# Attention by 256 tokens, weights in 1 MB pieces, second expert matrix and output in blocks of 320 and 192 columns

## The chip, the cores and the metric

One core of a Trainium2 chip runs the kernel. The metric is device time in microseconds (us) of one execution; lower is better. An execution of the kernel before took 193.95 us in the median of three runs (192.44 to 196.75).

## The reference

Chunked attention with memory keys, followed by a soft mixture of experts. Inputs are float32, and the sizes are: 4 batches, 8 heads, 768 tokens, head size 64; 3072 tokens of 512 channels for the experts; 8 experts with 4 slots each and 1024 hidden units.

```python
for c in range(nc):                                   # 24 chunks of 32 queries per batch
    k_ctx = k[:, :, max(0, 32*c - 16):min(S, 32*c + 32 + 8)]
    k_full = concatenate([mem_k, k_ctx], axis=2)      # 8 memory keys + at most 56
    a = softmax(scale * q_c @ k_full.T)
    out[:, :, c_start:c_end] = a @ v_full
x = out.transpose(0, 2, 1, 3).reshape(3072, 512)
logits = x @ phi                                      # 3072 x 32 slots
d = softmax(logits, axis=0)                           # over all tokens
slot_input = d.T @ x                                  # 32 x 512
for e in range(8):                                    # 4 slots of expert e
    slot_out[e] = relu(slot_input[e] @ w1[e]) @ w2[e] # 512x1024, then 1024x512
y = softmax(logits, axis=1) @ slot_out                # 3072 x 512
```

The inputs of the attention are 6.3 MB each for q, k and v, the two expert matrices 16.8 MB each, the output 6.3 MB.

## The kernel before, in words

**Attention.** `NU` = 24 units of 128 tokens. Of each unit, four chunks of 32 queries lie on the four column groups of TensorE, so that 16 matmuls of 128 columns make the scores (`s`, line 218), and 16 the product with the values (`a`, line 271). Two heads share the 128 partitions: even rows hold one head, odd rows the other, so every load of keys or values goes to every second partition (64 rows), once per head. Chunks overlap in their keys. The value windows of odd chunks have half of their keys in common with those of the even chunk: a copy on VectorE or ScalarE in turn (`share_v`, line 129) fills that half, in partitions 0 to 63, and a load of 32 rows (`vx`, in `load_v`, line 123) the other half, in partitions 64 to 127. Between the two products stand the row maximum, the subtraction, the exponential, the row sum and its reciprocal (VectorE and ScalarE), and transposes by TensorE (`pt`, and `xt` of the result for the logits). Every four units the logits (`l`, 16 matmuls of 128 columns) and the running sum over tokens (`D`, 4 matmuls of 512 columns) follow.

**Experts.** The slot inputs (`si`, copied to `siT`) are ready after the last unit. `expert_in` (line 484) multiplies them with `w1` of two experts at a time (`h`), `expert_out` (line 529) with one half of the columns of `w2` (`so`, 256 columns, two blocks). Between these stand the softmax over slots and its transposes (`combine_weights`, line 470, with a copy on GpSimd). `combine` (line 557) forms the output of one block (`o`), and six stores of 512 KB each write it.

**Transfers.** All of them are issued by SyncE (SP), in one order that the program fixes, and SP waits for each one's target buffer before it issues it; what stands behind waits as well. Weights come in pieces of 512 KB into `NW` = 13 buffers of their own during the attention (`load_w`, line 161, paced by `WRATE`), and into the attention's buffers as these are given up (`freed`, line 148). A piece can be loaded again into a buffer only when the piece before it has been used.

**Order of the work.** The loop over units (line 362) is written as a pipeline: in step `i` TensorE does the transposes of unit `i`, the scores of unit `i+2`, the result transposes of `i-1`, then the values of `i`. Each engine keeps the order in which its instructions are written (`InOrder`, line 56); the copies of GpSimd (POOL) at lines 115 and 473 do not belong to that rule. All instructions of a wrapped engine have the line of the helper (L66), so rows are told apart by the names of tiles.

Of the kernel before, what the change touches and what calls it, by code (L numbers as in the profile page):

```python
# [11 lines left out]
F32R = mybir.dt.float32r  # L12
# [4 lines left out]
P = 128  # L17
# [3 lines left out]
NKEY = NMEM + LEFT + CHUNK + RIGHT  # L21
CPU = P // CHUNK
UPB = S // P
NU = B * UPB
HALF_U = 3
NHALF = NU // HALF_U
SPAN_STEP = CPU // 2 * (NMEM + 2 * CHUNK)
SPAN_EXTRA = LEFT + RIGHT
STREAM = (S // CHUNK // 2) * (NMEM + 2 * CHUNK) + SPAN_EXTRA
HALF_W = HALF_U * SPAN_STEP + SPAN_EXTRA  # L30
# [3 lines left out]
E = 8  # L34
SPE = NSLOT // E
F = 1024
NG = NU // 4
NBLK = 2
WB = DM // NBLK
# [3 lines left out]
PIECE = 1024  # L43
NW = 13
NV = 3
W0 = 1
SHARE_MOD = 2
SHARE_DVE = 1
WARM0 = 3
FILL = (4, 2, 6, 2, 2)  # L50
WARM1 = 1
WRATE = 0.9
WSTART = 2


class InOrder:
    """An engine whose instructions keep the order in which they are written."""
# [13 lines left out]
def window_start(c):  # L71
    return (c // 2) * (NMEM + 2 * CHUNK) + (c % 2) * CHUNK


@with_exitstack
def tile_attn_softmoe(
# [3 lines left out]
    kT: bass.AP,  # L80
    vw: bass.AP,
    vx: bass.AP,
# [6 lines left out]
    pe, dve, act, sp = (InOrder(tc, e) for e in (nc.tensor, nc.vector, nc.scalar, nc.sync))  # L89
    cp = ctx.enter_context(tc.tile_pool(name="cp", bufs=1))  # L90
    wk = ctx.enter_context(tc.tile_pool(name="wk", bufs=2))
    ps = ctx.enter_context(tc.tile_pool(name="ps", bufs=2, space=bass.MemoryType.PSUM))

    k_slab = [cp.tile([P, 2, NPAIR, HALF_W], F32, tag=f"k{i}", name=f"k{i}") for i in range(2)]
    v_slab = [cp.tile([P, 2, 2, 2, 2, NPAIR, D], F32, tag=f"v{i}", name=f"v{i}") for i in range(NV)]
    q_slab = [cp.tile([P, 2, NPAIR, P], F32, tag=f"q{i}", name=f"q{i}") for i in range(3)]
    x_slab = [cp.tile([P, 4, DM], F32, tag=f"x{i}", name=f"x{i}") for i in range(2)]
    w_slab = [cp.tile([P, PIECE], F32, tag=f"w{i}", name=f"w{i}") for i in range(NW)]
    lT = cp.tile([P, NG, P], F32, tag="lT", name="lT")
    c_sb = cp.tile([P, NU, NSLOT], F32, tag="c", name="c_sb")  # L100
    hT = cp.tile([P, E, NFC, NSLOT], F32, tag="hT", name="hT")
# [4 lines left out]
    phi_sb = cp.tile([P, NKC, NSLOT], F32, tag="phi", name="phi_sb")  # L106

    def load_q(p):
        sp.dma_start(q_slab[p % 3], qT[p])

    def load_k(hb, lo=0, hi=HALF_W):
        b, half = divmod(hb, 2)
        off = half * HALF_U * SPAN_STEP - LEFT
        if half and lo == 0:
            nc.gpsimd.tensor_copy(
                out=k_slab[1][:, :, :, 0:SPAN_EXTRA], in_=k_slab[0][:, :, :, HALF_W - SPAN_EXTRA:HALF_W]
            )
        lo = max(lo, SPAN_EXTRA if half else LEFT)
        hi = min(hi, HALF_W - RIGHT if half else HALF_W)
        for par in range(2):  # L120
            sp.dma_start(k_slab[half][par:P:2, par, :, lo:hi], kT[b, :, par, :, off + lo:off + hi])

    def load_v(p):
        for par in range(2):
            sp.dma_start(v_slab[p % NV][par:P:2, par, 0], vw[p, par])
        for par in range(2):
            sp.dma_start(v_slab[p % NV][64 + par:P:2, par, 1], vx[p, par])

    def share_v(u):
        v = v_slab[u // 2 % NV]  # L130
        src, dst = v[64:128, :, 0, u % 2], v[0:64, :, 1, u % 2]
# [5 lines left out]
    flat = {}  # L137
    for name, tiles, pat in (
        ("k", k_slab, "p a g n -> p (a g n)"), ("q", q_slab, "p u g n -> p (u g n)"),
        ("v", v_slab, "p a o u c g d -> p (a o u c g d)"), ("x", x_slab, "p u n -> p (u n)"),  # L140
    ):
        for i, t in enumerate(tiles):
            f = t.rearrange(pat)
            flat[name, i] = [f[:, o:o + PIECE] for o in range(0, f.shape[1] - PIECE + 1, PIECE)]
    slabs = list(w_slab)
    last = NU // 2 - 1
    freed = [(NU - 6, ("k", 0)), (NU - 6, ("q", (last - 2) % 3)), (NU - 5, ("q", (last - 1) % 3))]
    freed += [(NU - 5, ("v", (last - d) % NV)) for d in range(NV - 1, 1, -1)]
    freed += [(NU - 3, ("q", last % 3)), (NU - 3, ("k", 1)), (NU - 3, ("v", (last - 1) % NV))]
    freed += [(NU - 1, ("x", 0)), (NU - 1, ("v", last % NV)), (NU, ("x", 1))]  # L150
    usable = {i: NW for i in range(NU + 1)}
    for since, key in freed:
        slabs += flat[key]
        for i in range(since, NU + 1):
            usable[i] = len(slabs)

    pieces = [("w1", e, kc) for e in range(E) for kc in range(NKC)]
    pieces += [("w2", blk, e, h) for blk in range(NBLK) for e in range(E) for h in range(2)]
    where = {}

    def load_w(upto):
        for i in range(len(where), min(upto, len(pieces))):
            kind, *at = pieces[i]
            where[pieces[i]] = s = slabs[i % len(slabs)]
            if kind == "w1":
                sp.dma_start(s, w1[at[0]].rearrange("(p kc) f -> p kc f", kc=NKC)[:, at[1], :])
            else:
                sp.dma_start(s, w2[at[0], at[1], :, at[2]])

    def span(t):  # L170
        lo = 0 if t == 0 else t * SPAN_STEP + SPAN_EXTRA
        return lo, (t + 1) * SPAN_STEP + SPAN_EXTRA

    warm = cp.tile([P, 512], F32, tag="warm", name="warm")

    def warm_up(n):
        w_ps = ps.tile([P, 512], F32, tag="L", name="warm_ps", bufs=1)
        for _ in range(n):
            pe.matmul(w_ps, lhsT=warm[:, 0:P], rhs=warm, start=True, stop=True)

    def keep_warm(n):
        if n:
            w_ps = ps.tile([P, 512], F32, tag="S", name="fill_ps")
            for _ in range(n):
                pe.matmul(w_ps[:, 0:P], lhsT=warm[:, 0:P], rhs=warm[:, 0:P], start=True, stop=True)

    dve.memset(warm, 0.0)
    for lo, hi in (span(0), (span(0)[1], HALF_W)):
        for par, eng in ((0, dve), (1, nc.gpsimd)):
            eng.memset(k_slab[0][:, par, :, lo:hi], 0.0)  # L190
    make_identity(nc, ident)
    for i in range(NV):
        nc.gpsimd.memset(v_slab[i], 0.0)  # L193
    nc.gpsimd.memset(hT, 0.0)
    act.copy(
        out=k_slab[1].rearrange("p a g n -> p (a g) n"),
        in_=warm[:, 0:HALF_W].rearrange("p (o n) -> p o n", o=1).broadcast_to([P, 2 * NPAIR, HALF_W]),
    )
    warm_up(WARM0)

    load_q(0)
    sp.dma_start(phi_sb, phi.rearrange("(kc p) s -> p kc s", p=P))
    load_k(0, *span(0))
    load_k(0, span(0)[1])
    load_q(1)
    load_v(0)
    load_k(1)
    for p in range(1, NV):
        load_v(p)
        if p == 1:  # L210
            load_q(2)
    load_w(W0)
    dve.tensor_reduce(out=sel, in_=ident.rearrange("p (g s) -> p s g", s=NSLOT), axis=AX.X, op=ALU.add)
    dve.tensor_copy(out=gsum, in_=sel.rearrange("p (o s) -> p o s", o=1).broadcast_to([P, 4, NSLOT]))

    pexp, rz, xT = {}, {}, {}

    def scores(u):
        t = u % UPB
        k = k_slab[(u // HALF_U) % 2]  # L220
        base = (t % HALF_U) * SPAN_STEP
        s_ps = ps.tile([P, H, NKEY], F32, tag="S", name=f"s{u}")
        for g in range(NPAIR):
            for j in range(CPU):
                w0 = base + window_start(j)
                pe.matmul(
                    s_ps[32 * j:32 * j + 32, 2 * g:2 * g + 2, :],
                    lhsT=q_slab[u // 2 % 3][:, u % 2, g, 32 * j:32 * j + 32],
                    rhs=k[:, :, g, w0:w0 + NKEY],
                    start=True, stop=True,  # L230
                )
        return s_ps

    def softmax(u, s_ps):
        t = u % UPB
        if t == 0:
            dve.memset(s_ps[0:32, :, 0:LEFT], NEG)
        if t == UPB - 1:
            dve.memset(s_ps[96:128, :, NKEY - RIGHT:NKEY], NEG)
        mx = wk.tile([P, H, 1], F32, tag="mx", name=f"mx{u}")  # L240
        dve.tensor_reduce(out=mx[:, :, 0], in_=s_ps, axis=AX.X, op=ALU.max)
        p = wk.tile([P, H * NKEY], F32, tag="p", name=f"p{u}", bufs=3)
        dve.tensor_tensor(
            out=p.rearrange("p (g n h) -> p g h n", g=NPAIR, h=2),
            in0=s_ps.rearrange("p (g h) n -> p g h n", h=2),
            in1=mx.rearrange("p (g h) o -> p g h o", h=2).broadcast_to([P, NPAIR, 2, NKEY]),
            op=ALU.subtract,
        )
        pexp[u] = p
# [367 lines left out]
```

## Time and profile before

| what | value |
|---|---|
| time of the runs | 192.44, 193.95, 196.75 us |
| span of the profiled execution | 193.7 us |
| TensorE busy, share of the span | 154.5 us, 80% |
| VectorE, ScalarE, GpSimd busy | 63%, 40%, 10% |
| bytes moved | 63.1 MB, of which 56.4 MB read from HBM and 6.3 MB written |
| mean rate | 326 GB/s |
| mean granted TensorE clock | 0.942 |

How to read it: busy shares are means over stages that have different limits, so they are read by stage, and against the row of the DMA engines. In that row the share is that of the 16 DMA engines that hold a packet, and GB/s is what they moved. A full share at a lower rate means packets that take longer, not more data. "issue" in a chain of waits is time in which the engine waited for nothing that the profile shows.

### The profile page before, as it was taken

The page shows a single profiled execution, that of the slowest core. Times are in us where ns is not written, and L with a number is a line of the kernel's source. Part 1 is how long each engine was busy: PE and PEld are TensorE (multiplying, and loading weights), DVE is VectorE, ACT ScalarE, POOL GpSimd, SP SyncE. Part 2 cuts the span into 40 slices and gives each one's busy share as a digit, 9 for nine tenths or more (in the row PEclk, how much of TensorE's full clock was granted, in tenths as well). Part 3 has the DMA queues.
Part 4 walks back from the last instruction along what each step waited for, and adds up shares of the span by engine and source line. Part 5 has one row for each costly group of instructions (what it writes and reads, how often), then busy time and mean ns, then how long its engine had stood idle before and what let it go on. Part 6 is the DMA issues. An engine that isn't in the chain of part 4 may idle for free.

```text
span 193.7 us, 6125 instructions
## 1 busy us (share of the span) xinstructions
PE 154.5 (80%) x2637; PEld 108.0 (56%) x2637; DVE 122.1 (63%) x249; ACT 77.9 (40%) x137; POOL 19.4 (10%) x22
## 2 busy tenths in 40 slices
PE   6733997859996969989579996999899769599540
PEld 3313775737684737757457684767466535365330
DVE  4699999829999649989936997243742220370550
ACT  8003457415756434763445577220322220160240
POOL 8991000000000000000000000000311100000000
PEclk9995899978999999999978999999999978999995
DMA  5999969998899999889978999999999999999296
GB/s 154 305 276 285 287 188 292 343 320 298 278 279 329 344 337 326 254 271 354 261 231 240 335 394 418 409 405 409 412 405 409 409 407 408 409 415 401 85 376 273
DMA packets 21194, 63.11 MB, mean 326 GB/s; under 512 B 2992, under 2 KB 7600, under 8 KB 21168
## 3 DMA queue, kind: packets, MB, share of 16 engines
q1 hardware_dynamic: 21168, 62.73, 92.8%
q8 instruction: 21, 0.34, 0.8%
q14 instruction: 5, 0.04, 0.1%
HBM read 56.43 MB, written 6.29 MB: 324 GB/s over the span
## 4 chain that ended last, share of the span: by engine, by line
PE 45%; DMA 23%; DVE 15%; issue 7%; POOL 3%; ACT 2%; SPq 1%; POOLq 0%
PE s L66 8%; PE a L66 8%; DMA k<-in_kT_dram 6%; DMA w<-in_w_dram 5%; PE xt_ps L66 5%; DMA v<-in_w_dram 5%; DVE z L66 4%; PE h L66 4%; PE so L66 4%; PE pt_ps L66 4%; DMA v<-in_vx_dram 3%; PE o L66 3%; PE D_ps L66 3%; DMA v<-in_vw_dram 3%; DVE v L66 3%
## 5 line engine op out<-in xcount | busy, mean ns | idle before, releaser
L66 PE MATMUL s<-k,q 128*32 128x128 f32 x768 | 28.8, 291 | 6.6 <-issue 4.2
L66 PE MATMUL a<-v,pt 128*32 128x128 f32 x768 | 27.8, 281 | 1.9 <-ACT pt L66 1.1
L66 PEld LDWEIGHTS s<-k,q 128*32 128x32 f32 x768 | 22.1, 117 | 12.1 <-issue 9.9
L66 PEld LDWEIGHTS a<-v,pt 128*32 128x32 f32 x768 | 21.4, 113 | 8.3 <-issue 6.4
L66 ACT COPY xT<-xt_ps 128x512 f32<-128x512 f32 x24 | 14.0, 584 | 29.2 <-PE xt_ps L66 28.9
L66 ACT ACTIVATE p<-p 128x512 f32<-128x512 f32 x24 | 15.1, 629 | 25.1 <-DVE p L66 25.1
L66 PE MATMUL pt_ps<-ident,p 128*128 128x128 f32 x96 | 16.7, 299 | 6.2 <-ACT p L66 6.2
L66 PE MATMUL xt_ps<-ident,x 128*128 128x128 f32 x96 | 16.4, 293 | 6.0 <-issue 4.4
L66 DVE TENSOR_TENSOR x<-a,z 128x512 f32<-128x512 f32 x24 | 16.5, 688 | 5.6 <-PE a L66 5.1
L66 DVE TENSOR_REDUCE mx<-s 128x8 f32<-128x512 f32 x24 | 16.1, 670 | 5.2 <-PE s L66 4.9
L66 PEld LDWEIGHTS pt_ps<-ident,p 128*128 128x128 f32 x96 | 10.7, 147 | 11.7 <-issue 11.7
L66 DVE TENSOR_TENSOR p<-s,mx 128x512 f32<-128x512 f32 x24 | 16.6, 693 | 0.8
L66 ACT COPY pt<-pt_ps 128x512 f32<-128x512 f32 x24 | 13.9, 578 | 8.0 <-PE pt_ps L66 8.0
L66 DVE TENSOR_REDUCE z<-p 128x8 f32<-128x512 f32 x24 | 16.3, 681 | 0.8
L66 PEld LDWEIGHTS xt_ps<-ident,x 128*128 128x128 f32 x96 | 10.4, 143 | 11.1 <-issue 7.5
L66 ACT COPY v<-v 64x1024 f32<-64x1024 f32 x12 | 12.5, 1046 | 0.3
L193 POOL MEMSET v<- 128x4096 f32 x3 | 10.5, 3513 | 0.0
L66 PE MATMUL o<-shl,cst 128*128 128x256 f32 x48 | 7.6, 302 | 3.0 <-DVE shl L66 2.9
L66 DVE COPY so_sb<-so 128x256 f32<-128x256 f32 x2 | 0.8, 425 | 14.1 <-PE so L66 14.1
L473 POOL COPY c<-c_sb 128x512 f32<-128x512 f32 x6 | 3.6, 614 | 60.3 <-DVE c_sb L66 48.0
L66 PEld LDWEIGHTS o<-shl,cst 128*128 128x128 f32 x48 | 6.3, 189 | 4.8 <-ACT shl L66 3.6
L66 PE MATMUL D_ps<-x,dT 128*32 128x512 f32 x48 | 7.4, 604 | 1.8 <-issue 1.6
(101 smaller groups left out, 195.1 us busy)
## 6 DMA issues: line engine op xcount, KB each, us to landing
w<-in_w_dram SPq DMA_DIRECT2D x26, 512.0 KB, 9.1
v<-in_w_dram SPq DMA_DIRECT2D x16, 512.0 KB, 10.2
q<-in_qT_dram SPq DMA_DIRECT2D x12, 512.0 KB, 7.2
v<-in_vw_dram SPq DMA_DIRECT2D x24, 256.0 KB, 6.6
k<-in_w_dram SPq DMA_DIRECT2D x12, 512.0 KB, 9.5
out_dram<-v SPq DMA_DIRECT2D x8, 512.0 KB, 5.2
k<-in_kT_dram SPq DMA_DIRECT2D x8, 424.0 KB, 8.5
v<-in_vx_dram SPq DMA_DIRECT2D x24, 128.0 KB, 6.7
```

The costliest lines, as they stand in the source:

```text
L66: return self.tc.keep_in_program_order(f(*args, **kwargs))
L193: nc.gpsimd.memset(v_slab[i], 0.0)
L473: nc.gpsimd.tensor_copy(out=c4, in_=c_sb[:, 4 * G:4 * G + 4, :].rearrange("p u (o s) -> p u o s", o=1).broadcast_to([P, 4, 4, NSLOT]),)
```

## The change

- A unit is 256 tokens (12 units). Scores and values stay 128 columns wide per matmul; the maximum, the exponential and the sums go over twice as many columns.
- The loads of keys bring one contiguous row of 4.5 to 4.7 KB per partition in place of four of 1.7 KB. They carry the part that two chunks share; the first chunk's keys are copied by GpSimd (`first_k`).
- The shared half of the odd chunks' values is copied by GpSimd (`share_v`, 8 copies of 256 columns per unit), no more by VectorE and ScalarE. The other half is a load of 32 rows to every fourth partition (`load_new`). Units 0 to 2 load both halves from memory (`load_both`).
- SP's order in a step is: `load_new` of unit `i+2`, even values of `i+4`, q of `i+4`, k of `i+5`, one piece of weights.
- Weights are pieces of 1 MB: 8 buffers of their own, then the attention's. The second matrix is cut at column 320: 11 pieces for the first block, 7 for the second, each 0.98 MB but for the last of a block.
- The logits of four units of 128 are formed as partial sums (4 matmuls of 512 columns, a copy, 4 matmuls of 128 columns). The last group keeps the old form.
- The softmax over slots of the first 12 units of 128 tokens is done under the last attention steps, the rest behind the first two experts, without the copies of GpSimd.
- The output of the first block is formed between the matmuls of the second block, and the combine matmuls read 32 rows each, in float32, in place of 128 rows in fp32r.

The core of the diff:

```diff
+U = 256
+UPB = S // U
+BLK = ((0, 320, 6), (320, 192, 10))
-PIECE = 1024
-NW = 13
+PIECE = 2048
+NB = 3
+NQ = 2
+NE = 4
+NO = 3
+NW = 8
+EARLY_W = 2
+WLAST = 7
...
-    def load_v(p):
-        for par in range(2):
-            sp.dma_start(v_slab[p % NV][par:P:2, par, 0], vw[p, par])
-        for par in range(2):
-            sp.dma_start(v_slab[p % NV][64 + par:P:2, par, 1], vx[p, par])
+    def load_v(u):
+        for h in range(2):
+            sp.dma_start(even_v(u)[h:P:2, h], vw[u, 64 * h:64 * h + 64, 0])
+    def load_both(u):
+        e, o = u % NE, NE + u % NO
+        for h in range(2):
+            sp.dma_start(v_t[h:P:2, e:o + 1:o - e, h], vw[u, 64 * h:64 * h + 64])
...
-        if u % SHARE_MOD < SHARE_DVE:
-            dve.tensor_copy(out=dst, in_=src)
-        else:
-            act.copy(out=dst, in_=src)
+        for h in range(2):
+            for i in range(CP):
+                cols = slice(NPAIR * D * i, NPAIR * D * (i + 1))
+                pool.tensor_copy(out=odd_v(u)[:, h, cols], in_=even_v(u)[:, h, cols])
+    def load_new(u):
+        for h in range(2):
+            sp.dma_start(odd_v(u)[h:P:4, h], vw[u, 64 * h:64 * h + 64:2, 1])
...
+    for u in range(NU - NB, NU):
+        freed += [(2 * u - 3, k_t[u % NB].rearrange("p a n -> p (a n)")[:, 0:PIECE])]
+    freed += [(2 * NU - 5, q_t.rearrange("p a g n -> p (a g n)"))]
+    freed += [(2 * u, even_v(u).rearrange("p a n -> p (a n)")) for u in range(NU - NE, NU)]
+    freed += [(2 * u, odd_v(u).rearrange("p a n -> p (a n)")) for u in range(NU - NO, NU)]
...
+    for i in range(NU):
+        if i and i + 2 < NU:
+            load_new(i + 2)
+        if i >= 1:
+            transpose_x(i - 1)
+        if i + 1 < NU:
+            exponent(i + 1)
...
+        a_ps = values(i, pt)
+        if G is not None and first:
+            lp = partial_logits(G)
...
+        normalize(i, a_ps)
+        if i + NE < NU:
+            load_v(i + NE)
+        if i >= WLAST:
+            load_w(usable[2 * i])
...
+        rest = (lambda: sum_logits(G, lp)) if G is not None and first else None
+        if i + 2 < NU:
+            softmax(i + 2, scores(i + 2, between=rest))
...
+        if i + 1 < NU:
+            pt = transpose_p(i + 1)
+            normalizer(i + 1)
+        if i + 3 < NU:
+            first_k(i + 3)
+            share_v(i + 3)
+        if i and i + 4 < NU:
+            load_q(i + 4)
+        if i + 5 < NU:
+            load_k(i + 5)
+        load_w(min(NW, EARLY_W + i) if i < WLAST else usable[2 * i + 1])
...
+    expert_out(0, banks("so0", "S")[:, 0, 0:BLK[0][1]])
+    under = {0: lambda: sum_sets(0)}
+    for G in range(NG - 1):
+        under[G + 1] = lambda G=G: combine(0, G, True)
+    expert_out(1, row(BLK[1][1], "so1"), under)
+    combine(0, NG - 1, True)
+    sum_sets(1)
+    for G in range(NG):
+        combine(1, G, G % 2 == 1)
```

**How it moves instructions.** First SP in the middle of the attention. Names: q, k and v are the attention's inputs, vw and vx the two kinds of value windows, w the weights. Before, over 256 tokens:

```order
L66 DMA v_67<-in_vw_dram 64x1024 x2
L66 DMA v_67<-in_vx_dram 32x1024 x2
L66 DMA q_71<-in_qT_dram 128x1024
L66 DMA w_76<-in_w_dram 128x1024
L66 DMA k_65<-in_kT_dram 64x4x424 x2
L66 DMA w_77<-in_w_dram 128x1024
```

And now, one step:

```order
L67 DMA v<-in_vw_dram 32x1024 x2
L67 DMA v<-in_vw_dram 64x1024 x2
L67 DMA q<-in_qT_dram 128x1024
L67 DMA k_66<-in_k_dram 64x1152 x2
L67 DMA w_74<-in_w_dram 128x2048
```

The load of 32 rows now stands first, ahead of the even values, and a piece of weights has twice the size. Next GpSimd in the same steps, where nothing but one copy of keys per six units stood before:

```order
L67 COPY k_66<-k_65 128x2x4x24
L67 COPY k_66<-k_66 128x2x4x8
L67 COPY v<-v 128x256 x8
L67 COPY k_67<-k_66 128x2x4x24
L67 COPY k_67<-k_67 128x2x4x8
L67 COPY v<-v 128x256 x8
```

It has nine or ten copies per step, and `load_new` waits for the eight of its unit. Last TensorE near the end; so is the second matrix's product, r its sum over the four column groups, o the output. Before:

```order
L66 MATMUL so_2323<-k_65,hT 32x256 x12
L66 MATMUL r_2390<-so_sb_2388,gsum 128x256
L66 MATMUL o_0_0_2396<-shl_2392,cst_1992 128x256 x2
L66 MATMUL o_0_1_2400<-shl_2392,cst_1992 128x256 x2
L66 MATMUL o_1_0_2405<-shl_2392,cst_2052 128x256 x2
```

And now, inside the second block:

```order
L67 MATMUL so_2071<-v,p 32x192 x8
L67 MATMUL o_3_S<-xT,lT 128x320 x2
L67 MATMUL o_3_A<-xT,lT 128x320 x2
L67 MATMUL so_2071<-k_66,p 32x192 x8
L67 MATMUL o_4_S<-xT,lT 128x320 x2
L67 MATMUL o_4_A<-xT,lT 128x320 x2
L67 MATMUL so_2071<-k_66,p 32x192 x2
```

The first block's output now lies between the matmuls of the second block, where it stood ahead of all of them.

## Rows read from the trace of the kernel before

**Rows 1.** The page's 40 slices of the span: DMA share in tenths, rate.

```profile
DMA  5999969998899999889978999999999999999296
GB/s 154 305 276 285 287 188 292 343 320 298 278 279 329 344 337 326 254 271 354 261 231 240 335 394 418 409 405 409 412 405 409 409 407 408 409 415 401 85 376 273
```

**Rows 2.** Busy time by stage, us: PE, PEld, DVE, ACT, POOL; clock, DMA share, GB/s.

```profile
0.00:20.00 20.00, 11.24 (x104) 6.00 (x108) 15.43 (x15) 6.30 (x5) 14.69 (x13) 0.85 0.91 258
20.00:112.00 92.00, 78.71 (x1649) 58.65 (x1641) 74.10 (x159) 47.54 (x85) 1.04 (x3) 0.96 0.93 293
...
139.00:172.00 33.00, 28.44 (x381) 17.65 (x381) 11.01 (x26) 8.97 (x17) 2.46 (x4) 0.95 1.03 408
...
180.00:184.00 4.00, 2.43 (x14) 1.85 (x14) 2.14 (x5) 1.42 (x3) 0.00 (x0) 1.00 0.11 44
184.00:193.70 9.70, 2.08 (x14) 1.60 (x12) 2.57 (x4) 2.37 (x5) 0.00 (x0) 0.71 0.82 324
```

**Rows 3.** The same columns, short stretches inside the attention, by what was queued.

```profile
9.60:10.60 1.00, 1.00 (x29) 0.75 (x21) 1.00 (x1) 0.00 (x0) 1.00 (x2) 1.00 1.07 418
20.00:21.00 1.00, 1.00 (x28) 0.92 (x24) 0.93 (x4) 0.00 (x0) 0.00 (x0) 0.55 1.12 389
43.00:45.00 2.00, 2.00 (x26) 1.47 (x28) 1.66 (x3) 0.65 (x2) 0.00 (x0) 0.55 1.06 393
64.00:66.00 2.00, 2.00 (x53) 1.44 (x44) 1.43 (x3) 0.58 (x1) 0.00 (x0) 1.00 1.04 410
16.60:17.90 1.30, 0.35 (x2) 0.38 (x3) 1.26 (x3) 0.63 (x1) 0.00 (x0) 0.50 1.00 186
21.20:22.40 1.20, 1.20 (x30) 0.83 (x26) 1.17 (x3) 0.15 (x1) 0.00 (x0) 1.00 0.98 198
```

**Rows 4.** The page's DMA issues: count, KB each, median us to landing.

```profile
v<-in_vx_dram SPq DMA_DIRECT2D x24, 128.0 KB, 6.7
```

**Rows 5.** Chain of waits, 45 to 57 us: start, us, what; one unit's matmuls.

```profile
45.55 0.59 PE pt_ps L66 x4
...
46.25 1.01 PE s L66 x32
47.26 0.59 PE xt_ps L66 x4
47.84 1.01 PE a L66 x32
...
51.05 1.00 PE D_ps L66 x8
```

**Rows 6.** The same chain, 26 to 45 us: a wait for keys and the logits.

```profile
28.76 4.29 DMA k<-in_kT_dram
...
37.78 1.01 PE l L66 x32
```

**Rows 7.** The same chain, 122 to 194 us: end of the attention to the experts.

```profile
122.26 0.88 PE a L66 x32
...
132.90 0.29 DVE siT L66
...
139.07 3.59 PE h L66 x64
...
172.46 7.09 PE so L66 x128
```

**Rows 8.** Timeline from 0 to 24 us: start, us, engine, line, what.

```profile
6.25 6.96 POOL L193 MEMSET v<- 128x4096 f32 x2
...
20.27 1.36 PE L66 MATMUL a<-v,pt 128*32 128x128 f32 x32
```

**Rows 9.** Groups of instructions by form: busy us, mean ns, idle time before.

```profile
L66 DVE COPY gsum<-sel 128x128 f32<-128x128 f32 x1 | 8.3, 8291 | 0.0
...
L473 POOL COPY c<-c_sb 128x512 f32<-128x512 f32 x6 | 3.6, 614 | 60.3 <-DVE c_sb L66 48.0 <-PE ct_ps L66 12.3
...
L115 POOL COPY k<-k 128x192 f32<-128x192 f32 x4 | 1.4, 346 | 73.4 <-DMA k<-in_kT_dram 73.4
```

More of the change, by code (lines that the diff above doesn't have):

```diff
@@ L148, in tile_attn_softmoe @@
[L148 to L154, printed above, removed]
+    stats = cp.tile([P, 3, NG], F32, tag="stats", name="stats")
+    warm = cp.tile([P, P], F32, tag="warm", name="warm")
@@ L159, in tile_attn_softmoe @@
+    pieces += [("w2", blk, i) for blk, (_, _, per) in enumerate(BLK) for i in range(-(-E * NFC // per))]
+    first_w2 = {blk: pieces.index(("w2", blk, 0)) - 2 * E for blk in range(len(BLK))}
     where = {}
@@ L191, in tile_attn_softmoe @@
[L191 to L230, printed above, removed]
-                )
-        return s_ps
@@ L251, in exponent, with clear_k, clear_v @@
-    def exponent(u):
-        act.activation(out=pexp[u], in_=pexp[u], func=AF.Exp, scale=SCALE)
+                _, n, per = BLK[at[0]]
+                n *= min(per, E * NFC - per * at[1])
+                sp.dma_start(s[:, 0:n], w2[first_w2[at[0]] + at[1], :, 0:n])
+    def clear_k(eng, u, h, part=slice(0, KW)):
+        eng.memset(k_t[u][:, h, part], 0.0)
+    def clear_v(eng, t, halves=range(2)):
+        for h in halves:
+            if eng is act:
+                act.copy(out=t[:, h], in_=warm[:, 0:1].broadcast_to([P, VW]))
+            else:
+                eng.memset(t[:, h], 0.0)
@@ new lines, in tile_attn_softmoe @@
+    dve.memset(warm, 0.0)
+    for h in range(2):
+        clear_k(dve, 0, h, slice(0, KW // 2))
+        clear_k(pool, 0, h, slice(KW // 2, KW))
+    clear_k(dve, 1, 0)
+    clear_k(pool, 1, 1)
+    for u in range(NDIRECT):
+        clear_v(act, even_v(u))
+    clear_v(dve, odd_v(0), [0])
+    clear_v(pool, odd_v(0), [1])
+    clear_k(dve, 2, 0)
+    clear_k(pool, 2, 1)
+    load_q(0)
+    load_q(1)
+    load_k(0)
+    load_k(1)
+    load_both(0)
+    load_q(2)
+    load_k(2)
+    first_k(0)
+    clear_v(dve, odd_v(1), [0])
@@ new lines, in transpose_x, with partial_logits @@
+    def transpose_x(u, between=None):
+        for s in range(NSUB):
+            if s and between:
+                between()
+            t_ps = row(512, f"xt_ps{u}_{s}")
+            for kc in range(NKC):
+                pe.transpose(t_ps[:, P * kc:P * kc + P], x_of(u)[:, s, P * kc:P * kc + P], ident)
+            act.copy(out=xT[:, :, 2 * (u % 2) + s, :], in_=t_ps.rearrange("p (kc n) -> p kc n", kc=NKC))
+    def partial_logits(G):
+        l_ps = row(512, f"lp{G}")
+        for kc in range(NKC):
+            pe.matmul(
+                l_ps[32 * kc:32 * kc + 32, :],
+                lhsT=phi_sb[:, kc, :],
+                rhs=xT[:, kc].rearrange("p g n -> p (g n)"),
+                start=True, stop=True,
+            )
+        lp = wk.tile([P, 512], F32, tag="lp", name=f"lp_sb{G}", bufs=1)
+        act.copy(out=lp, in_=l_ps)
+        return lp
@@ L531, in expert_out @@
+    def expert_out(blk, tile, after={}):
+        _, n, per = BLK[blk]
         for e in range(E):
[L532 to L533 removed]
+            for q in range(2):
                 for j in range(4):
+                    i, at = divmod(8 * e + 4 * q + j, per)
                     pe.matmul(
[L536 to L540 removed]
@@ new lines, in _layouts, with windows @@
+    vs = stream(v, inputs["mem_v"]).reshape(B, NPAIR, 2, STREAM, D // NKC, NKC).swapaxes(-1, -2).reshape(B, NPAIR, 2, STREAM, D)
+    def windows(first):
+        rows = np.array([[[STEP * (CP * u + i) + r for i in range(CP)] for u in range(UPB)] for r in first])
+        w = vs[:, :, :, rows]
+        return w.transpose(0, 4, 2, 3, 5, 1, 6).reshape(NU, 2 * len(first), CP, NPAIR * D)
+    even = [CHUNK * (r % 2) + r // 2 for r in range(2 * CHUNK)]
+    odd = [CHUNK * (2 - r % 2) + r // 2 for r in range(2 * CHUNK)]
@@ new lines, in _layouts @@
+    vw = np.stack([windows(even), windows(odd)], axis=2)
+    phi = inputs["moe_phi"].reshape(P, NKC, NSLOT)
+    w2 = []
+    for start, n, per in BLK:
+        c = inputs["moe_w2"].reshape(E * NFC, P, DM)[:, :, start:start + n].swapaxes(0, 1)
+        for i in range(0, E * NFC, per):
+            part = c[:, i:i + per].reshape(P, -1)
+            w2.append(np.pad(part, ((0, 0), (0, PIECE - part.shape[1]))))
+    w2 = np.stack(w2)
+    return {"qT": qT, **kT, "vw": vw, "phi": phi, "w1": inputs["moe_w1"], "w2": w2}
```

636 lines of the change are left out of this document (340 added, 296 removed).

## The prediction

> **What bounds the kernel now.** The first view is the page's row of slices [rows 1]. The DMA share is nine tenths or full nearly everywhere, but the rate has two levels: some 230 to 360 GB/s up to the 23rd slice, that is 111 us, and 400 to 418 after it. So the transfers are the thing to count, and in the first part they are slow without being idle. The second view is busy time by stage [rows 2]. From 20 to 112 us TensorE is busy for 78.7 of 92 us and the DMA engines have a share of 0.93 at 293 GB/s; from 139 to 172 us the share is 1.03 at 408. A full share reads 1.03 here, so the first part lacks a tenth of its time to an empty queue, and the rest to packets that take longer: 293 x 1.03 / 0.93 = 324 GB/s would be its rate with a queue that is never empty. From 180 to 184 us hardly anything moves (44 GB/s): the first block's stores are done, and the second block's result does not exist yet.
>
> The third view says which packets are slow [rows 3]. By the order of issue the queue's head held even value windows (64 rows) in the first two stretches, keys mostly in the third, weights in the fourth: 418, 389, 393 and 410 GB/s at a full share. In the last two it held the 32-row value loads of partitions 64 to 127: 186 and 198 GB/s, at a full share as well. There are 24 of those [rows 4].
>
> The chain of waits gives TensorE's own pace. One unit of 128 tokens without a wait costs 0.59 (`pt`) + 1.01 (`s`) + 0.59 (`xt`) + 1.01 (`a`) = 3.20 us; the running sum of four units costs 1.00 us [rows 5], their logits 1.01 [rows 6]. That makes 24 x 3.20 + 6 x 2.01 = 89 us. The values of the first unit began at 20.3 us [rows 8], those of the last ended at 123.1 [rows 7]; of this attention some 14 us or more are waits, for example 4.3 us for keys [rows 6].
>
> **The sum: transfers.** The change moves q 6.3 MB, k 12 x 0.59 = 7.1, values by 64 rows 3 x 1.05 + 9 x 0.52 = 7.9 and by 32 rows 9 x 0.26 = 2.4, together 23.6 MB (22.8 before); then weights 33.6 and the output 6.3. I first ask whether the queue can stay full, and then price the bytes.
>
> Queue: in one step SP issues 0.26 + 0.52 + 0.52 + 0.59 + 1.05 = 2.95 MB, or 7.4 to 8.2 us at 400 to 360 GB/s. TensorE needs 2 x 3.20 = 6.40 us per step, and per two steps 1.00 for the running sum and 1.25 for the logits (4 matmuls of 512 columns at the price of the running sum's four, and a quarter of 1.01 for the 4 of 128 columns): 7.5 us per step. The two are near each other, and the start puts a stock before them: SP can issue q and k of three units and both halves of two units' values, 5.4 MB, before it must wait for the first scores. So I take the queue as never empty in the attention.
>
> At its end, TensorE must give back weight buffers in time. The first values start at about 15 us. Ahead of them stand, one behind the other: q of two units and k of the first, 1.65 MB, at 258 GB/s with some 1 us to begin, till 7.5 us; GpSimd's copy of its keys, 0.35, three memsets of 1024 columns at 6.96 / 8 = 0.87 us each [rows 8], and two copies more, till 11.2; the scores of the second unit, 2.0, and the transposes, 1.2, till 14.4, and their copy. Up to there 5.2 us of TensorE's 12 x 6.40 + 5 x 2.25 = 88 us are done, and 1.2 us (the last `xt`) come after, so the last values end at 15 + 88 - 6.4 = 97 us. From the last values to `siT` it was 133.2 - 123.1 = 10.1 us, and two experts take 3.6 [rows 7]: at 111 us the first four pieces are given back. Till then 21 buffers can be filled; with the rates below, that takes till 122 us. TensorE is 11 us ahead, which covers waits of the kind seen before. The same slack is why I cost the following at nothing: 0.25 us more for the logits of each group, the memsets of the start (on three engines, while the first loads land), and larger VectorE instructions. VectorE and ScalarE lose `share_v` and the per-instruction cost of half of their reductions; that gives nothing either, because they are not what the sum waits for. Without that cover each of these would count in full.
>
> At the end, the first block's output is formed inside the second block. TensorE's work there is 7.09 x 192 / 256 = 5.3 us [rows 7] plus 24 output matmuls: 6 x 0.63 = 3.8 us if four run beside each other like those of the running sum, 15 us if they do not. Loads of the second block (6.3 MB) and stores of the first (3.9 MB) last 25 us, so either is hidden, and the 4 us of 180 to 184 [rows 2] go: the first block's stores stand directly behind the last load, and 9.6 us of them cover the second block's last matmuls, its sum and first copies. What is late next is the store queue itself.
>
> Price, in us. Weights and output: 39.9 MB at 408 GB/s = 97.8. q at 410: 15.3. k at 393: 18.1 (rows of 4.6 KB in place of 1.7 KB should not be slower). Values by 64 rows at the mean of 418 and 389: 19.6. Start: the first slice moved 154 x 4.84 = 0.75 MB, so 3.0 us are lost [rows 1]. End: 184 to 193.7 us moved 324 x 9.7 = 3.1 MB, so 2.0 us are lost [rows 2]. The unknown is the 32-row load, now on every fourth partition. Like 64 rows it costs 2.4 / 0.40 = 5.9; like the 32 rows of before 2.4 / 0.192 = 12.3. The nearest row is the one of the same number of rows, so I take 12.3. Sum: 97.8 + 15.3 + 18.1 + 19.6 + 12.3 + 3.0 + 2.0 = 168.1 us. With 5.9 it is 161.7.
>
> The Trainium skill ("SBUF — State Buffer", Door 1: The DMA port swizzle) says that a transfer is as fast as the ports that its partitions reach, and that partitions 64 to 127 reach 8 of 16. By that rule the trace agrees (186 and 198 beside 389 to 418), and every fourth partition would reach all ports, which makes the sum 161.7. The rows cannot tell the number of rows from their place, so I stay with the slower price.
>
> The span of the profiled execution is 193.7 us, 0.25 below the runs' median; I forecast **168 us**.
>
> **Rivals.**
>
> *1. The slow mixture stays.* In 20 to 112 us it was not only the 32-row loads that were slow, since 324 GB/s is below what 3.1 MB at 190 explain (27.0 MB at 405 and of these 2.8 at 190 give 360). If their neighbours suffer as before, the 23.6 MB and the 8 pieces go at 324: 32.0 / 0.324 = 98.8, the rest 31.5 / 0.408 = 77.2, with 5.0 for the ends **181 us**. For it: that rate. Against it: 389 to 418 where the 32-row loads are not at the head [rows 3].
>
> *2. The queue runs empty again.* SP waits in order: `load_new` waits for GpSimd, and values, q, k and weights stand behind it. If a tenth of the time is lost as before, the 98.8 us of rival 1 become 109: **191 us**. Against it: the stock of 5.4 MB, and an order from SP that has 2.95 MB in every step.
>
> *3. Slower: GpSimd and VectorE shut each other out.* Each step has 8 copies of 256 columns and up to 2 of keys on GpSimd. Copies there took 614 ns for 512 columns and 346 for 192 [rows 9], so some 3.2 to 3.5 us per step. VectorE has 74.1 us in 92 [rows 2], that is 6.9 per 256 tokens, or 6.2 without its `share_v`. If they took turns, a step would last 9.6 us in place of 7.5; over the 9 steps with copies TensorE would end 19 us later, 8 us past its lead: 176. It decides only if a step exceeds about 12 us (copies of 0.58 us, or VectorE waiting for whole runs of them): then TensorE is 41 us late, 30 past its lead, and the time is **198 us or more**. For it: a VectorE copy beside GpSimd's memsets took 8.29 us [rows 9]. Against it: VectorE's maxima, subtractions and scalings read PSUM, and GpSimd's run starts after the values, when VectorE is in just those. The Trainium skill ("SBUF — State Buffer", SBUF: two separate sides) speaks against this change here: GpSimd and some VectorE instructions take one pair of ports, the whole instruction long. The 8.29 us agree with it; applied to all of VectorE it gives the 176, to those that it names less.
>
> **How the numbers follow.** Forecast 0.72, rival 1 0.16, rival 2 0.08, rival 3 0.04. The range runs from the fast price of the 32-row load to rival 1: 161 to 181. A measurement of this kernel tells about 2% from no change, so faster is below 190.1 and slower above 197.8. Faster: 0.72 + 0.16 + 0.03 of rival 2 = 0.91. Same: the rest of rival 2 and a little of rival 3, 0.06. Slower: 0.03.
>
> **What would show it.** The DMA share should read full from 10 us to the end, with no stretch like 180 to 184; the rate in the attention 350 to 400 GB/s and 408 after it. TensorE's last values should end near 97 us and the experts' first product start near 107. GpSimd's copies should take 0.3 to 0.35 us, and no VectorE instruction should be longer than its fellows beside them. The forecast is wrong if the share has holes behind `load_new`, if stretches with 32-row loads are as slow as before together with their neighbours, or if the first product starts after 120 us.

## The result and the profile after

The changed kernel takes **166.37 us** in the median of four runs (164.84 to 166.87); the kernel before, on the same chip, 193.89 us. The ratio is 0.868, with a 95% interval of 0.859 to 0.878. Executions of one kernel fall into a faster and a slower group, a few per cent apart; ratios, and the times of the experiments below, are of the faster ones, to which all four of the kernel after belong. The forecast was 168 us. The profiled execution took 166.87 us with a span of 165.1.

The first view is again the page's row of slices of the kernel after, the DMA share in tenths and the rate:

```profile
DMA  5999999999999999999998899999999999999894
GB/s 196 325 404 413 418 415 412 424 407 420 404 405 382 400 417 407 415 385 399 399 395 267 311 425 413 428 406 393 386 411 415 401 420 419 426 387 405 351 397 180
```

Before, the rate was 188 to 354 GB/s from the second slice up to 111 us and about 400 only behind that, with a hole in the 38th slice [rows 1]. Now it is about 400 from the third slice on. The hole is gone; another, shallower one stands in slices 22 and 23.

By stage (after; PE, PEld, DVE, ACT, POOL busy, then clock, DMA share, GB/s):

```profile
0.00:10.00 10.00, 7.73 (x74) 4.37 (x74) 6.00 (x9) 7.05 (x7) 7.12 (x15) 1.00 0.81 281
10.00:80.00 70.00, 60.62 (x1363) 51.06 (x1359) 54.68 (x95) 31.80 (x59) 29.94 (x86) 0.98 1.01 407
80.00:94.00 14.00, 10.59 (x253) 8.30 (x246) 9.30 (x20) 5.07 (x11) 2.80 (x8) 1.00 0.92 338
94.00:110.00 16.00, 14.81 (x244) 11.21 (x243) 12.96 (x29) 8.67 (x20) 1.81 (x1) 1.00 1.01 417
110.00:140.00 30.00, 29.19 (x426) 16.36 (x428) 6.24 (x25) 4.95 (x10) 0.00 (x0) 1.00 1.01 407
140.00:160.00 20.00, 16.86 (x248) 8.79 (x240) 9.10 (x17) 7.71 (x17) 0.00 (x0) 0.98 0.97 393
160.00:165.10 5.10, 0.00 (x0) 0.00 (x0) 0.00 (x0) 0.00 (x0) 0.00 (x0) 0.50 0.55 218
```

**Where the time came from.** Rate times length gives the bytes. Before, 20 us at 258 and 92 us at 293 GB/s [rows 2] moved 32.1 MB by 112 us. After, 10 us at 281, 70 at 407 and 1.9 at 420 moved the same 32.1 MB by 82 us. The rest, 31.0 MB before and 31.8 after, took 82 and 83 us. So the gain of 28.6 us of span lies in the first half of the bytes, in their rate. The hole before the second block's stores went too, about 4 us [rows 2], but the bytes behind the first half are 0.8 MB more (2 us), and 80 to 94 us lost 2.5 us against 412 GB/s.

The chain of waits of the kernel after (start, us, what), to be set beside [rows 7]:

```profile
14.60 1.95 PE a L67 x64
...
82.27 3.01 issue
...
102.78 1.88 PE a L67 x64
...
113.83 0.30 DVE siT L67
...
118.77 3.59 PE h L67 x64
...
131.37 16.39 DMA v<-in_w_dram
...
151.21 1.44 PE so L67 x32
...
158.12 0.56 DVE w L67
```

The first values begin at 14.6 us (20.3 before, [rows 8]), the last end at 104.7 (123.1 before), `siT` comes at 113.8 (132.9 before). From 131 us on TensorE waits for weights: there the transfers set the time alone, and the last output is formed 6 us before the end, while stores run.

### The profile page after: what moved, and what is told of

The parts are those of the page before. It is cut to its first block, busy times and chain, and to the rows that moved or that the text cites. A ratio compares the mean times of both kernels' runs of the same rounds, so it can differ in the third digit from the quotient of the medians.

```text
span 165.1 us, 6050 instructions
## 1 busy us (share of the span) xinstructions
PE 139.8 (85%) x2583; PEld 100.1 (61%) x2583; DVE 98.3 (60%) x190; ACT 65.2 (40%) x123; POOL 41.7 (25%) x109
## 4 chain that ended last, share of the span: by engine, by line
PE 55%; DVE 14%; DMA 13%; issue 8%; ACT 4%; POOL 2%; ACTq 0%; POOLq 0%; DVEq 0%; SPq 0%
PE s L67 11%; DMA v<-in_w_dram 10%; PE a L67 10%; PE h L67 9%; PE xt_ps L67 5%; PE pt_ps L67 5%; PE D_ps L67 4%; DMA k<-in_k_dram 3%; DVE p L67 3%; DVE mx L67 3%; PE lp L67 2%; PE o_S L67 2%; ACT p L67 2%; PE l L67 1%; DVE x L67 1%
## 5 line engine op out<-in xcount | busy, mean ns | idle before, releaser
L67 POOL COPY v<-v 128x256 f32<-128x256 f32 x72 | 25.2, 400 | 31.7 <-DMA v<-in_vw_dram 16.0
L67 DVE TENSOR_TENSOR p<-s,mx 128x512 f32<-128x512 f32 (+1 forms) x26 | 15.8, 654 | 0.4
L67 ACT ACTIVATE p<-p 128x1024 f32<-128x1024 f32 (+1 forms) x13 | 12.9, 994 | 7.8 <-DVE p L67 7.8
L67 DVE TENSOR_REDUCE mx<-s 128x16 f32<-128x1024 f32 (+1 forms) x13 | 14.8, 1141 | 1.7 <-PE s L67 1.4
L67 DVE TENSOR_REDUCE z<-p 128x16 f32<-128x1024 f32 x12 | 14.6, 1215 | 0.0
L67 POOL COPY k<-k 128x192 f32<-128x192 f32 (+2 forms) x20 | 5.6, 290 | 11.5 <-DMA k<-in_k_dram 11.2
L67 PE MATMUL D_ps<-x,dT 128*32 128x512 f32 (+1 forms) x56 | 7.1, 539 | 1.6 <-ACT dT L67 1.6
L67 PE MATMUL h<-w,siT 128*32 128x256 f32 x128 | 7.5, 381 | 0.4 <-DVE siT L67 0.4
L67 PE MATMUL so<-w,p 128*32 128x320 f32 (+1 forms) x108 | 7.1, 395 | 0.0
L67 PE MATMUL o_S<-xT,lT 32*128 32x320 f32 (+1 forms) x36 | 6.5, 438 | 0.6
```

The source lines that it names most:

```text
L67: return self.tc.keep_in_program_order(f(*args, **kwargs))
```

## The experiments

Each kernel is the kernel after with one edit, unless the text says "before". Differences are to the 166.37 us of the kernel after. A ratio is to the kernel before as it was run beside the experiment, 190.6 to 192.9 us.

**The place of the 32 rows, undone.**

```diff
-            sp.dma_start(odd_v(u)[h:P:4, h], vw[u, 64 * h:64 * h + 64:2, 1])
+            sp.dma_start(odd_v(u)[64 + h:P:2, h], vw[u, 64 * h:64 * h + 64:2, 1])
```

> The changed kernel, with its 32-row value loads sent to every second partition from 64 up, as the kernel before sent them (the rows land in other places than the product reads, the bytes are the same). Theory A, the place of the rows sets their rate: 18 loads of 0.131 MB go from about 0.32 to 0.68 us each, so at least 6.4 us more than the 166.4 us of the changed kernel, 172 to 175, more if the loads queued beside them slow down too, and stretches near 200 GB/s come back. Theory B, the rate goes with the number of rows or came from a queue that ran empty: within 1.5 us of 166.4.

Measured: 179.43 us, ratio 0.941 (0.929 to 0.953), so 13 us slower. Two stages of its profiled execution, which took 181.69 us (the kernel after has 399 and 401 GB/s in the same two):

```profile
40.00:60.00 20.00, 16.37 (x355) 13.76 (x346) 11.53 (x20) 6.82 (x14) 7.73 (x24) 0.93 1.02 327
60.00:80.00 20.00, 16.51 (x384) 13.71 (x381) 15.77 (x29) 8.31 (x17) 7.79 (x24) 1.00 1.02 328
```

Same bytes, same number of rows, a full share, and a fifth less rate. The place of the rows decides, not their number. And 2.36 MB cannot lose 13 us at the slow price alone: at 192 instead of 400 GB/s they lose 6.4. The transfers queued beside them became slower as well: if only the 0.26 MB of these loads in a step went at 192 and the other 2.69 MB at 400, the step's rate would be some 365 GB/s, not 327.

**The place alone, put into the kernel before.**

```diff
-            sp.dma_start(v_slab[p % NV][64 + par:P:2, par, 1], vx[p, par])
+            sp.dma_start(v_slab[p % NV][par:P:4, par, 1], vx[p, par])
```

> The kernel before, with its 32-row value loads sent to every fourth partition, as the changed kernel sends them (the rows land in other places than the product reads; the copies of the shared half now also wait for them). Theory A, the place sets the rate: 24 x 0.36 = 8.6 us less transfer time, so about 185 us, down to 175 if the loads beside them recover too. Theory B: the attention of the kernel before was paced by engines and waits, so 190 to 195.

Measured: 183.71 us in one execution and 186.52 to 189.66 in three others, beside 189.75 to 196.43 for seven of the kernel before. The two ranges do not meet, and the difference is some 7 us. Two of its stages:

```profile
20.00:40.00 20.00, 17.79 (x402) 13.77 (x395) 17.82 (x40) 11.03 (x17) 0.35 (x1) 0.94 0.71 246
40.00:60.00 20.00, 18.02 (x402) 13.63 (x401) 18.07 (x38) 11.99 (x24) 0.35 (x1) 0.99 1.00 358
```

Where the queue is full the rate is now 358 GB/s; but the queue runs empty (share 0.71), because TensorE and VectorE are busy for 18 of 20 us and SP waits for them, 26.4 us for TensorE's value products alone from 14 to 100 us. So the place alone brings a quarter of the gain. What keeps the 358 below the 400 of the kernel after was not tried apart: the rows of keys, the size of the pieces and the units differ as well.

**More work for TensorE.** The scores of one half of each unit are computed twice, 12 us more.

```diff
-            for g in range(NPAIR):
+            for g in [*range(NPAIR), *range(NPAIR if s == 0 else 0)]:
```

> The changed kernel, with the scores of the first 128 tokens of each unit computed twice: 1.0 us more TensorE work in each of 12 units, no byte more. Theory A, transfers bound it and TensorE has some 4 to 11 us of lead: 0 to 7 us more, 166 to 173. Theory B, the engines' chain bounds the attention: 12 us more, 178.

Measured: 181.74 us, ratio 0.953 (0.937 to 0.969): 15.4 us slower for 12 us of work. Its attention:

```profile
20.00:110.00 90.00, 74.93 (x1766) 63.84 (x1768) 58.44 (x101) 35.57 (x69) 29.25 (x87) 0.98 0.93 345
```

`siT` comes at 128.4 us, 14.6 later. A lead of 11 us would have left 1 to 4 us of this. There was no lead. The rest above 12 us is not work: the list of TensorE's waits has 16.0 us of "issue" between 14 and 113 us, where the kernel after has 9.8; the last section says what these are.

**Less work for TensorE.** The transposes of the result and their copies are left out in units 2 to 10, 7.8 us less.

```diff
+            if 2 <= u < NU - 1:
+                continue
```

> The changed kernel without the transposes of the attention's result and their copies in units 2 to 10 (the logits then read stale columns): 0.87 us less TensorE work and 1.2 us less ScalarE work in each of 9 units, 7.8 us of TensorE in all, no byte less. Theory A, the transfers alone bound it and TensorE has a lead: 165 to 167 us. Theory B, after the run with more scores: TensorE's pace releases the buffers that the queue waits for, and it has no lead, so the time falls with it, to 158 to 161. Bytes set a floor of 63.5 / 0.415 + 3 + 2 = 158 us.

Measured: 165.90 us, ratio 0.862 (0.850 to 0.875), which cannot be told from the kernel after. Its attention, and the chain's row of `siT`:

```profile
20.00:100.00 80.00, 64.29 (x1436) 49.88 (x1434) 61.80 (x110) 30.48 (x59) 29.08 (x87) 0.98 1.02 407
```

```profile
111.58 0.30 DVE siT L67
```

7.8 us less work brought `siT` forward by only 2.2, and the queue is full, a share of 1.02. Little of the rest is TensorE waiting for data: its list of waits from 14 to 113 us has 0.5 us for values, but 12.2 us of "issue" (9.8 in the kernel after) and 2.0 for ScalarE's copy of `pt` (0.2). So TensorE's pace and the queue meet almost exactly. More work costs at once, less gains nothing.

**The shared values copied by VectorE and ScalarE in turn**, as before, in place of GpSimd.

```diff
-                pool.tensor_copy(out=odd_v(u)[:, h, cols], in_=even_v(u)[:, h, cols])
+                if u % 2:
+                    dve.tensor_copy(out=odd_v(u)[:, h, cols], in_=even_v(u)[:, h, cols])
+                else:
+                    act.copy(out=odd_v(u)[:, h, cols], in_=even_v(u)[:, h, cols])
```

> The changed kernel with the 72 copies of shared values put back on VectorE and ScalarE in turn, by units, in place of GpSimd. Theory A, the copies' engine is hidden: 165 to 168 us. Theory B, moving them to GpSimd is a part of the gain, since VectorE and ScalarE stand between TensorE's products: 8 copies of some 0.3 us in a step, 9 steps, 1.6 to 2.4 us each, so 172 to 186. Theory C, GpSimd's copies delay the 32-row loads and all that stands behind them on SP: faster, 160 to 164.

Measured: 170.65 us from two executions (169.88 and 171.41; the two others took 172.87 and 173.16), some 4 us slower, between the first two theories. The queue empties once:

```profile
80.00:100.00 20.00, 17.89 (x390) 14.33 (x392) 16.81 (x34) 12.64 (x28) 0.00 (x0) 1.00 0.82 279
```

The copies do lie on the path when they stand in VectorE's and ScalarE's order: in this stretch the chain of waits has one run of eight of them on ScalarE, 2.55 us from 81.2.

**Both halves from memory.** All odd values are loaded whole by 64 rows; GpSimd's 72 copies are gone.

```diff
-            sp.dma_start(odd_v(u)[h:P:4, h], vw[u, 64 * h:64 * h + 64:2, 1])
+            sp.dma_start(odd_v(u)[h:P:2, h], vw[u, 64 * h:64 * h + 64, 1])
-            share_v(i + 3)
```

> The changed kernel, but the odd chunks' values of units 3 to 11 are loaded whole, 64 rows of 4 KB per head in place of 32 rows, and GpSimd's 72 copies of the shared half are gone. That is 9 x 0.26 = 2.36 MB more to move. Theory A (transfers set the pace and GpSimd's copies are hidden): 2.36 MB at 408 GB/s make it 5.8 us slower, 172 us, with a full share from 20 to 110 us. Theory B (the copies and SP's waits behind them cost something too, as the holes between 80 and 94 us could mean): 166 to 169 us. Theory C (a load of 32 rows to every fourth partition costs more than its bytes, 12.3 us in place of 5.9 for all of them, as the forecast's sum took it): then the load of 64 rows costs no more than that of 32, and the time is 166 us or less.

Measured: 169.09 us, ratio 0.884 (0.879 to 0.890): 2.7 us slower for 2.36 MB more, where the bytes alone are 5.8. One of its stages (0.94 and 363 GB/s in the kernel after), and VectorE's subtractions in the kernel after and then in this one (form, count, busy us, mean ns, idle before):

```profile
80.00:100.00 20.00, 17.24 (x356) 13.45 (x345) 15.87 (x30) 8.83 (x18) 0.24 (x1) 1.00 1.02 412
```

```profile
L67 DVE TENSOR_TENSOR p<-s,mx 128x512 f32<-128x512 f32 x22 | 14.3, 697 | 0.4
```

```profile
L67 DVE TENSOR_TENSOR p<-s,mx 128x512 f32<-128x512 f32 x22 | 14.3, 700 | 0.4
```

The subtractions are as long with GpSimd's copies beside them as without, and so are the maxima (1223 ns in both): VectorE's large instructions and the copies do not lock each other out here. One small instruction does show it, the scaling of the row sums (count; ns least, median, most; the kernel after, then this one):

```profile
L67 DVE TENSOR_SCALAR z<-z x12: 174/176/366, 17.1 to 103.1; 128x16 f32<-128x16 f32 x12
L67 DVE TENSOR_SCALAR z<-z x12: 174/175/177, 16.6 to 102.2; 128x16 f32<-128x16 f32 x12
```

In the kernel after, three of the twelve take 345 to 366 ns, each of them beside work of GpSimd: a memset, a copy of values, a copy of keys; it is some 0.5 us in all.

The queue stays full up to 120 us, so some 3 us of the kernel after belong to its copies, to SP's waits behind them, or to its hole at 82 us, where TensorE waited for 3.0 us and in this kernel for 1.9; the split is not settled. The price of 12.3 us for the 32-row loads is excluded: the 64 rows in their place, 4.7 MB, cost 11.7 at the forecast's own 404 GB/s, and this kernel would have been no slower.

**No weights before step 7.**

```diff
-        load_w(min(NW, EARLY_W + i) if i < WLAST else usable[2 * i + 1])
+        load_w(usable[2 * i + 1] if i >= WLAST else 0)
```

> The changed kernel with no piece of weights before step 7: the 8 pieces of 1 MB that went into the attention's first seven steps come behind it. Theory A, the queue is the bound: steps 0 to 6 then carry 1.9 MB in some 7.3 us, 260 GB/s, the rest of the queue's time is lost, and 8.4 / 0.41 = 20 us come later, less what the attention gains: 178 to 187 us. Theory B, weights in the attention delay keys and values, and TensorE is what counts: at most 170.

Measured: 176.47 us, ratio 0.918 (0.909 to 0.927): 10 us slower. The queue without weights to fill it:

```profile
20.00:40.00 20.00, 18.70 (x437) 15.31 (x438) 17.67 (x28) 10.54 (x19) 9.58 (x29) 1.00 0.80 291
40.00:60.00 20.00, 17.90 (x408) 14.81 (x402) 15.78 (x28) 10.09 (x20) 10.23 (x31) 1.00 0.93 337
```

TensorE is then the slower side for a while, and the weights are paid later. It is less than 8.4 MB at 408 GB/s (20.6 us), since the attention first gets its inputs sooner: the logits that wait until 85.3 us in the kernel after go on at 78.7. But the edit does not spread the eight pieces, SP issues them in one run from 68.6 us, ahead of the last `q`:

```profile
76.58 18.70 DMA q<-in_qT_dram
```

TensorE waits 10.1 us for it, and `siT` comes at 118.9 us, 5.1 later than in the kernel after. So the 10 us are the price of this order, not of late weights alone.

**The first block's output not woven in,** but formed before the second block's matmuls.

```diff
-    under = {0: lambda: sum_sets(0)}
-    for G in range(NG - 1):
-        under[G + 1] = lambda G=G: combine(0, G, True)
-    expert_out(1, row(BLK[1][1], "so1"), under)
-    combine(0, NG - 1, True)
+    sum_sets(0)
+    for G in range(NG):
+        combine(0, G, True)
+    expert_out(1, row(BLK[1][1], "so1"))
```

> The changed kernel with the first block's output formed ahead of the second block's matmuls, as in the kernel before. The second block's matmuls, 5.3 us, and its sum then come after all six groups of the first block, while 9.6 us of stores are queued. Theory A, the store queue covers it: 165 to 168 us. Theory B, a hole like the one from 180 to 184 us of the kernel before comes back: 169 to 172.

Measured: 174.49 us, ratio 0.907 (0.895 to 0.919): 8.1 us slower, more than either theory had. Stage and chain:

```profile
150.00:160.00 10.00, 8.91 (x112) 5.02 (x116) 1.77 (x3) 1.43 (x3) 0.00 (x0) 0.58 0.53 215
```

```profile
153.99 7.58 PE so L67 x128
```

The second block's matmuls now come as one piece behind the last combine, and half of them find no store beside them. It is the hole of before [rows 2] come back, wider: SP issues no store between 155.3 and 164.3 us. Some 2 us of it are the granted clock of 0.58, since the 7.6 us would be the forecast's 5.3 at the full clock; TensorE had waited between small combines just ahead, busy for 5.4 of the 10 us before 150.

**Two equal blocks** of 256 columns.

```diff
-BLK = ((0, 320, 6), (320, 192, 10))
+BLK = ((0, 256, 8), (256, 256, 8))
```

> The changed kernel with the second matrix and the output cut into two equal blocks of 256 columns, as before, in place of 320 and 192. The bytes are the same. Behind the last load then stand 3.1 MB of the first block's stores (7.7 us at 408 GB/s) in place of 3.9 MB (9.6 us), and the second block's own work is a third longer: its last matmuls, sums and copies. Theory A (the stores of the first block cover the second block's end, and the queue stays the bound): 165 to 168 us. Theory B (the end is set by the second block's chain from its last weight to its last store): 1.8 us more of TensorE's work behind the last weights and 0.8 MB more of stores after the last output, 2.0 us, so 169 to 171 us.

Measured: 167.02 us, ratio 0.872 (0.865 to 0.878), the same as after. The unequal cut brings nothing that can be measured; the weaving does.

**No filler matmuls** between the attention and the experts.

```diff
-FILL = (1, 3, 3, 2, 2)
+FILL = (0, 0, 0, 0, 0)
```

> The changed kernel without the eleven filler matmuls that TensorE runs between its last attention unit and the experts, where it would otherwise wait for the other engines. Theory A (transfers set the time, and the buffers are given back early enough either way): 165 to 168 us, with the first expert product starting at 112 to 114 us. Theory B (the way from the last values to the first expert product sets when weight buffers come free): up to 2 us faster, 164 us. Theory C (without the filler TensorE's granted clock is at its lower level when the experts begin, and the first two experts take longer): the first four groups of expert products take 7 us each in place of 3.6, but the buffers come free early enough for the queue only if the loss stays below the lead; 168 to 175 us.

Measured: 169.19 us, ratio 0.883 (0.875 to 0.891), 2.8 us slower, at the edge of what the intervals can tell. The chain at the first experts, and the stage:

```profile
113.03 1.08 PE h L67 x8
...
114.64 5.42 PE h L67 x56
...
120.53 3.59 PE h L67 x64
```

```profile
113.00:125.00 12.00, 11.97 (x145) 6.10 (x149) 3.40 (x12) 1.90 (x3) 0.00 (x0) 0.74 0.84 316
```

`siT` came 1.1 us earlier, but TensorE had stood idle in places (busy for 1.9 us from 110 to 113), its granted clock fell to the lower of its two levels from 113 to 119 us (0.74 in the mean of this stretch), the first two experts took 6.5 us in place of 3.8, and the buffers came back late (share 0.84). Only the first group was slow, not four.

**Every q loaded twice**, meant as 6.3 MB more.

```diff
     def load_q(u):
         sp.dma_start(q_of(u), qT[u])
+        sp.dma_start(q_of(u), qT[u])
```

> The changed kernel, with every load of q issued twice: 6.3 MB more in the attention, nothing more for the engines. Theory A, the transfers bound the whole kernel: 6.3 / 0.41 = 15.4 us more, 178 to 183 us. Theory B, the larger units have shortened the engines' chain and transfers hide under it: at most 5 us more.

Measured: 215.86 us, ratio 1.136 (1.109 to 1.163). As a test of bytes it failed: the second load of a buffer waits until the first has landed, and SP issues nothing meanwhile. SP's longest waits:

```profile
SPq L67 <- DMA q<-in_qT_dram: 63.8, 11, 7.0
```

It shows something else twice over. Eleven waits on SP of 5.8 us in the mean, 64 us in all, made it 49 us slower, 34 more than the bytes. And TensorE's "issue" waits are absent from it, see below.

## Why the prediction was right, and where not

**What bounds it: right.** The share is full and the rate near 400 GB/s from 10 us on, but for the hole at 82; the whole gain lies in the rate of the first half.

**The price of the 32 rows: wrong by the forecast's choice.** The sum took 12.3 us where the runs show the full rate, which makes it 5.9: the same number of rows is slow in partitions 64 to 127 and at full rate on every fourth partition. With 5.9 the forecast's sum is 161.7. The Trainium skill ("SBUF — State Buffer", Door 1: The DMA port swizzle) says that the bandwidth of a transfer depends on how many ports its partitions reach. The trace agrees, 407 GB/s from 10 to 80 us with these loads in the queue. That the neighbours slow down too (13 us, not 6.4) is what the first experiment adds.

**"TensorE is 11 us ahead": the step that failed.** The forecast had the last values end at 97 us, `siT` at 107 and the buffers full at 122, and let the 11 us cover both "waits of the kind seen before" and several small terms. The values ended at 104.7, `siT` came at 113.8. TensorE's work was not counted too low: from the first values (14.6 us) to the last it took 90.1 us, of which these were waits without a releaser, by the list of waits of the kernel after, 14 to 105 us (total, times, longest):

```profile
PE s L67 <- issue: 4.3, 4, 2.0
PE l L67 <- issue: 3.0, 1, 3.0
PE a L67 <- issue: 2.5, 5, 0.8
```

That is 9.8 us, and 90.1 - 9.8 = 80.3 is beside the 82 of the forecast (2.9 us of waits for other engines are still in it). The same kind of wait stood in the kernel before, and the forecast did not count it. By its list from 20 to 123 us:

```profile
PE xt_ps L66 <- issue: 4.4, 2, 3.8
PE s L66 <- issue: 4.2, 3, 2.4
PE D_ps L66 <- issue: 1.6, 1, 1.6
...
PE a L66 <- issue: 0.8, 1, 0.8
```

11.0 us there. The 9.8 us of the kernel after use up the lead of 11 but for about 1. The other end of that lead, the buffers full at 122, was too late as well: it rests on the slow price of the 32 rows, and with 5.9 it is 115.6. With `siT` 6.7 us after its forecast no lead is left, which is what the two TensorE runs show from both sides (+15.4 us for 12 more, nothing for 7.8 less).

**"The queue is never empty": nearly.** The longest of these waits, 3.0 us at 82.3, holds the scores behind it; SP waits for them for 5.8 us, and slices 22 and 23 are the hole: 2.5 us.

**The sum, by terms.** With the fast loads 161.7; the hole adds 2.5, and 140 to 160 us at 393 GB/s 0.9; the ends lose 3.2 and 2.4 instead of 3.0 and 2.0. That makes 165.7 beside a span of 165.1. Around the span lie 1.8 us; the forecast set the profiled span of before 0.25 below the median and so took it as the whole. The 6.4 us too much for the 32 rows and some 5 us not counted nearly cancel. That 168 lies within 2 us of 166.4 is luck, two wrong terms of opposite sign; that the transfers bound the kernel is not.

**The end: right, by the weaving.** The stores follow the last load as forecast, and without the weaving 8.1 us are lost. The cut at 320, from which the forecast worked out its 9.6 us of cover, does not matter: 7.7 us of cover do as well.

**GpSimd's copies: hardly a lock, but dearer than taken.** After:

```profile
L67 POOL COPY v<-v 128x256 f32<-128x256 f32 x72 | 25.2, 400 | 31.7 <-DMA v<-in_vw_dram 16.0 <-PE pt_ps L67 5.5 <-PE D_ps L67 3.6
L67 POOL COPY k<-k 128x192 f32<-128x192 f32 x8 | 2.8, 345 | 0.0
```

The forecast halved 614 ns for 512 columns and got 0.31 to 0.35 us. A line through 345 at 192 and 614 at 512 [rows 9] gives 399 at 256, the measured value: a fixed part of 184 ns does not halve. Rival 3 is refuted by the equal durations of VectorE's large instructions; of the sign that no VectorE instruction should be longer than its fellows, only the small scaling failed. Rival 1 is what the first experiment looks like: 327 GB/s, the 324 of its rate, when the rows are put back, and its time, 179.4 beside 181.

## What to carry to other kernels

Count what a slow transfer does to those queued beside it, not only its own bytes: moving 32 rows over all partitions was worth some 7 us alone and 13 us where the queue was always full. A lead of one engine over another must contain that engine's unexplained waits, which the list of waits has as "issue", before it may cover other costs. And parts of such a change do not add up: taken out one at a time, weights early (10 us), weaving (8), GpSimd's copies (4) and the place (13) make 35 us, where the whole gained 28. Only the place was also tried alone.

## What the runs showed of the hardware that was not expected

**TensorE's "issue" waits stand at the same instructions from run to run, and end with a packet of instructions.** The long ones, in the kernel after (its third, 3.01 us at 82.27, stands in the chain above), in that with both halves from memory and in that with equal blocks, whose TensorE programs are alike up to there:

```profile
40.65 1.96 issue
...
74.79 1.42 issue
```

```profile
40.90 1.87 issue
...
74.74 1.42 issue
82.22 1.91 issue
```

```profile
40.88 1.60 issue
...
48.47 2.33 issue
...
74.81 1.42 issue
82.30 1.91 issue
```

The wait at 48.47 has no long fellow in the other two: at the same matmul they wait for 0.24 and 0.41 us. So the place is fixed and the length is not. Counted along TensorE's matmuls, these places are some 126 apart, and no "issue" wait of the list in these three kernels stands elsewhere.

The page lists a queue of twenty 16 KB instruction packets:

```profile
q8 instruction: 20, 0.33, 0.8%
```

In the trace of the kernel after and in those of all experiments on it, each "issue" wait of TensorE behind 14 us, 91 of them, ends 1.2 to 1.6 us after one of these packets has ended, whether it lasted 0.19 or 3.17 us; so do 9.2 of the 11.0 us before. The wait of 3.01 us, which makes the hole at 82 us, ends at 85.28, and its packet ran from 82.91 to 83.91. In the kernel that loads q twice, with the same TensorE program and the same twenty packets but a DMA share of 0.81 from 20 to 130 us, the list has no "issue" at all: there TensorE, held up by q, reaches each of the places 1.4 us or more after the end of its packet. So TensorE waits for its own instructions. Why their packets come late is argued, not tried by itself: between TensorE's passing one place and the start of the packet for the next lie 3.6 to 6.7 us in the kernel after from 17 to 85 us, at a full share, and 0.1 to 1.4 us in three cases of other kernels where the share in between was below 0.4. That fits packets that stand behind data in the queue. It costs some 10 us of TensorE's time here, and a kernel with more matmuls meets more of it: with the scores computed twice there are 23 packets and 16.0 us.

**A clock that falls costs a queue.** Leaving out eleven filler matmuls cost 2.8 us, because the first two experts, at a granted clock of 0.50 up to 119 us, give their buffers back late.
